# A third transfer buffer for the weights' conversion, an earlier and thinner interleaving of the first mixture, and phi(q) on ScalarE

## The chip, the cores and the metric

The kernel runs on one core of one Trainium2 chip. A core has TensorE (PE: matrix products; PEld is its weight load), VectorE (DVE), ScalarE (ACT), GpSimd (POOL) and SyncE (SP), which here issues nearly all transfers. They run in parallel, each through its own list of instructions in a fixed order, and wait for one another on semaphores. The metric is the time of one execution on the device, in microseconds (us), lower is better; the times before are three runs, of which the median counts.

## The reference

Three layers follow each other. Attention over 2 batches of 8 heads, 576 tokens and 64 columns per head joins causal softmax attention with a lookup in a memory through phi(q). Then comes a dense mixture layer with a piecewise quadratic activation, then a top-1 mixture of 8 experts with a capacity:

```
scores = where(causal, -1e9, (q @ k.T) / 8)          # per batch and head
local  = softmax(scores) @ v
phi(x) = where(x > 0, x, exp(x) - 1) + 1
mem    = (phi(q) @ M_prev) / (phi(q) @ z_prev + 1e-6)
x      = g * mem + (1 - g) * local                    # g = sigmoid(beta), x: [1152, 512]
h      = x @ w_in                                     # [1152, 2048]
x      = where(h >= 1, h, where(h <= -1, 0, (h + 1)**2 / 4)) @ w_out
e      = argmax(x @ w_gate)                           # 8 experts, capacity 288
out    = gate * (relu(x @ w1[e]) @ w2[e])
```

`w_in` and `w_out` arrive as 64-bit numbers, and the kernel converts them itself.

## The kernel before

**Attention** (`attn`) goes through 40 chunks of up to 128 queries for two heads at once. The first 20 are of batch 0 (first two chunks for each of four head pairs, then three for each), the last 20 of batch 1. A step of the generator is one third of an iteration: `softmax(i)` (scores on PE, maximum on DVE at L306 or L320, exponential on ACT at L308 or L324, reciprocal on DVE at L331, scaling on POOL at L336 and ACT at L334), then `turn(i - 1)` (transposes on PE at L355, copies on ACT at L356), then `values(i - 3)` (products with v on PE at L381; the finished block goes to `XT` on ACT at L385 and DVE at L386). `prep_a` loads a head pair, and splits keys and queries into two planes on POOL (L245) and DVE (L250). `prep_b` computes phi(q) in the tile `pf` (ACT at L262, DVE at L263 and L264) and its products with the memory on PE (L268), which need a bank of the pool `ps_m`. The tokens of the first block (`XT[0]`, 256 tokens) are ready after step 33, those of the second (`XT[1]`, 320 tokens) after step 69, and there are 129 steps.

**The weights' conversion** (`load_half`) has 8 pieces for each of four halves. A piece is a transfer of 512 KB into a buffer of the pool `st` (SP, L164), three instructions on DVE (L170 to L172, into a tile `ws`, which has two buffers), and a high and a low plane on ACT (L173) and POOL (L174). The last reader of an `st` buffer is L172; after it SP may issue the next transfer into that buffer.

**The first mixture**: `moe0(bi)` takes a block through the first half of the layer: eight steps of `layer1` (12 products at L429 into a bank of `ps_m`; ACT at L436 and L439, DVE at L437, L438 and L440), then four steps of 24 products with `w_out` (L446) and a store. Blocks 0 and 1 are interleaved with attention. Blocks 2 and 3 (`moe0s`) follow it, beside the conversion of the second halves, whose space is free only when attention's tiles are.

The order in which an engine gets its instructions is set before the run: `mix(a, b, ra, rb)` takes ra steps of a and rb steps of b in turn, and a scheduler then places each instruction by its own estimate of when its inputs are there. On the chip nothing changes place any more, so an instruction that waits holds everything behind it on its engine. `m` and `hp` are banks of `ps_m`, of which there are two.

Of the kernel before, what the change touches and what calls it, by code (L numbers as in the profile page):

```python
# [13 lines left out]
AF = mybir.ActivationFunctionType  # L14
ALU = mybir.AluOpType
# [37 lines left out]
def f(ap):  # L53
    return ap.bitcast(F32)
# [3 lines left out]
def kernel(ctx: ExitStack, tc: tile.TileContext, kd, kq_d, qx_d, v_d, mz_d,  # L58
                              betap, betab, w_in, w_out, w_gate, w1, w2, cap, out):
    nc = tc.nc  # L60
    ACT, DVE, POOL, PE, SP = nc.scalar, nc.vector, nc.gpsimd, nc.tensor, nc.sync
# [15 lines left out]
    def bank(p, tag):  # L77
        return p.tile([128, 512], F32, tag=tag, name=tag)
# [45 lines left out]
    def setup_late():  # L124
        POOL.memset(wg, 0.0)
        SP.dma_start(out=wg[:, :, :NE], in_=w_gate.rearrange("(k p) e -> p k e", p=128))

        for e in range(2):
            o = 2 * e * FEW
            DVE.tensor_tensor(out=summing[:, e * FEW:(e + 1) * FEW], in0=ident[:, o:o + FEW],  # L130
                              in1=ident[:, o + FEW:o + 2 * FEW], op=ALU.add)
        POOL.memset(onesb, 1.0)
        POOL.memset(upper, 1.0)
        POOL.affine_select(out=upper, in_=upper, pattern=[[1, 128]], compare_op=ALU.is_gt,
                           fill=0.0, base=0, channel_multiplier=-1)
        for e in range(NE):
            POOL.memset(rev[:, e:e + 1], float(NE - e))
# [7 lines left out]
    def wtile(slot, j, planes=True):  # L145

        shape, dt = ([128, 2, 4, 512], F32R) if planes else ([128, 4096], F32)
        return pools[slot].tile(shape, dt, tag=f"w{slot}{j}", name=f"w{slot}{j}")

    def load_half(half, key):  # L150

        if key == "in":
            src = w_in.bitcast(I32)[:, half * 2048:(half + 1) * 2048].rearrange("(k p) f -> p k f", p=128)
        else:
            src = w_out.bitcast(I32)[half * 1024:(half + 1) * 1024, :].rearrange("(k p) d -> p k d", p=128)
        ts = [wtile(slot_of[key, half], j) for j in range(2)]
        wt[key, half] = ts
        for i in range(8):  # L160
            j, k = divmod(i, 4)
            t = ts[j]
            r = st.tile([128, 512, 2], I32, tag="st", name="st")
            d = SP.dma_start(out=r.rearrange("p a b -> p (a b)"),  # L164
                             in_=src[:, k, j * 1024:(j + 1) * 1024] if key == "in" else src[:, i, :])
            if (key, half) == ("in", 0) and i < NPIN:
                tc.keep_in_program_order(d)
            lo, hi = r[:, :, 0], r[:, :, 1]
            s = tp.tile([128, 512], I32, tag="ws", name="ws")
            DVE.tensor_scalar(s, hi, 3, 0x3FFFFFFF, op0=ALU.logical_shift_left, op1=ALU.bitwise_and)  # L170
            DVE.scalar_tensor_tensor(out=s, in0=hi, scalar=-0x40000000, in1=s, op0=ALU.bitwise_and, op1=ALU.bitwise_or)  # L171
            DVE.scalar_tensor_tensor(out=s, in0=lo, scalar=29, in1=s, op0=ALU.logical_shift_right, op1=ALU.bitwise_or)  # L172
            ACT.activation(out=t[:, 0, k, :], in_=f(s), func=AF.Copy)  # L173
            POOL.tensor_tensor(out=t[:, 1, k, :], in0=f(s), in1=f(t[:, 0, k, :]), op=ALU.subtract)  # L174
            yield

    def rows_of(n):

        return [(r, c0, c1) for r, c0, c1 in ((128, 0, 2), (64, 2, n)) if c0 < c1]
# [18 lines left out]
    def qcols(a, b):  # L198
        return slice(a, b) if b <= CUT else slice(S + a, S + b)

    def attn(P):
# [51 lines left out]
        def prep_b(vi, si):  # L253

            b, pr, subs = visits[vi]
            t = T[vi]
            mz = t["mz"]
            sub = SUBS[si]
            q0, q1 = CH[sub[0]][0], sum(CH[sub[-1]])
            qr = t["kq"][:, qcols(q0, q1)]  # L260
            pf = qp.tile([128, 320], F32, tag="pf", name="pf", bufs=1)[:, :q1 - q0]
            ACT.activation(out=pf, in_=qr, func=AF.Exp)  # L262
            DVE.tensor_scalar(pf, pf, 1.0, None, op0=ALU.min)  # L263
            DVE.scalar_tensor_tensor(out=pf, in0=qr, scalar=0.0, in1=pf, op0=ALU.max, op1=ALU.add)  # L264
            nps = bank(ps_m, "m")
            for i, ci in enumerate(sub):
                o, m = CH[ci]
                PE.matmul(nps[:m, i * 130:i * 130 + 130], pf[:, o - q0:o - q0 + m], mz, start=True, stop=True)  # L268
            nv = nps[:, :390].rearrange("p (c x) -> p c x", c=3)
            rn = mp.tile([128, 3, 2], F32, tag="rn", name="rn")  # L270
            xm = mp.tile([128, 3, 128], F32, tag="xm", name="xm")
            for r, c0, c1 in rows_of(len(sub)):
                gb = gall[:r, 2 * pr:2 * pr + 2].unsqueeze(1).to_broadcast([r, c1 - c0, 2])
                DVE.scalar_tensor_tensor(out=rn[:r, c0:c1], in0=nv[:r, c0:c1, 128:130], scalar=1.0e-6, in1=gb, op0=ALU.add, op1=ALU.mult)
                DVE.reciprocal(rn[:r, c0:c1], rn[:r, c0:c1])
                DVE.tensor_tensor(out=xm[:r, c0:c1].rearrange("p c (h d) -> p c h d", h=2),  # L276
                                  in0=nv[:r, c0:c1, :128].rearrange("p c (h d) -> p c h d", h=2),
                                  in1=rn[:r, c0:c1].unsqueeze(3).to_broadcast([r, c1 - c0, 2, 64]), op=ALU.mult)
            t["xm", si] = xm
# [339 lines left out]
    def head(g, n):  # L619
        for _ in range(n):  # L620
            if next(g, 0) == 0:
                return
            yield

    def mix(a, b, ra, rb):

        a, b = iter(a), iter(b)
        la = lb = True
        while la or lb:
            for _ in range(ra):  # L630
                la = la and next(a, 0) != 0
            for _ in range(rb):
                lb = lb and next(b, 0) != 0
# [302 lines left out]
    side = ExitStack()  # L936
# [1 line left out]
    def spool(name, bufs):  # L938
        return side.enter_context(tc.tile_pool(name=name, bufs=bufs, side="right"))

    st = ctx.enter_context(tc.tile_pool(name="st", bufs=2, side="right"))
    g1 = ExitStack()
    ga = pool("ga", GA)
    gb = g1.enter_context(tc.tile_pool(name="gb", bufs=5))
# [2 lines left out]
    cmask2 = P[2].tile([128, 64], BF16, name="cmask2", bufs=1)  # L947
    setup(cmask, cmask2)
    at = attn(P)
    mix(head(at, 39), chain(load_half(0, "in"), load_half(0, "out")), 5, 2)  # L950
    setup_late()
    route_init()
    m0 = moe0(0)
    mix(head(at, 24), head(m0, 8), 3, 1)
    mix(head(at, 12), m0, 4, 1)
    m1 = moe0(1)
    mix(at, head(m1, 9), 9, 1)
    m0 = chain(moe0s(2, ga), moe0s(3, ga))
    next(m0)
    run(m1)  # L960
# [101 lines left out]
```

## Time and profile before

| what | value |
|---|---|
| median of 3 runs (lowest, highest) | 452.03 us (449.75, 453.09) |
| the profiled execution's own time | 446.63 us |
| its span | 444.9 us |
| PE busy | 410.1 us, 92% of the span |
| DVE, ACT, POOL busy | 289.6, 208.2, 140.2 us |
| mean granted clock of TensorE | 0.969 of full speed |

The trace comes from one execution. The slices of the page show PE at nine tenths or more after some 245 us, and below that in the first half, where attention, the first mixture and the conversion run side by side; the clock that was granted falls to a half for some microseconds in a few places there. Busy time of PE includes the modelled ends of its products, so a busy PE isn't yet a PE at its peak.

### The profile page before, as it was taken

The numbers are of one execution on the slowest core, as the hardware profiler recorded it, in microseconds if no ns is written. First come the engines' busy times: TensorE is split into PE (matmuls) and PEld (weight loads), VectorE is DVE, ScalarE is ACT, GpSimd is POOL, SyncE is SP. The second block draws the span as 40 slices with busy tenths as digits, with TensorE's granted clock in tenths as the row PEclk, the third lists the DMA queues.
The fourth block names the chain that finished last, engine by engine and source line by source line (L and its number), as shares of the span: only waits on it lengthen the run. The fifth ranks groups of instructions, "written<-read, shape, count | busy, mean of one in ns | idle before, by whom it ended". The sixth has DMA issues, their size and how long they took to land. (4 is left out here: it accounts for less than half of the span.)

```text
span 444.9 us, 8598 instructions
## 1 busy us (share of the span) xinstructions
PE 410.1 (92%) x3023; PEld 343.8 (77%) x3024; DVE 289.6 (65%) x921; ACT 208.2 (47%) x587; POOL 140.2 (32%) x161
## 2 busy tenths in 40 slices
PE   8997878979699999999888999999989999999993
PEld 4553565857488787888887999998987989989951
DVE  5459979898957877588789444445554756557230
ACT  3667664868543877674334323223444323132121
POOL 4127748665633252144425000000276200200002
PEclk9899968999899999999969999999999999999998
DMA  4176772846576540006542300300544303993001
GB/s 124 50 230 219 245 245 87 325 138 226 165 249 250 159 133 7 2 18 194 172 151 96 96 1 1 118 1 25 166 147 163 96 1 133 334 315 134 14 1 56
DMA packets 30414, 58.79 MB, mean 132 GB/s; under 512 B 3549, under 2 KB 15197, under 8 KB 30370
## 3 DMA queue, kind: packets, MB, share of 16 engines
q1 hardware_dynamic: 27986, 49.44, 34.2%
q0 software_dynamic: 2384, 8.80, 6.1%
q8 instruction: 24, 0.39, 0.3%
q14 instruction: 20, 0.16, 0.1%
HBM read 50.53 MB, written 7.80 MB: 131 GB/s over the span
## 5 line engine op out<-in xcount | busy, mean ns | idle before, releaser
L429 PE MATMUL hp<-xt,win 128*128 128x256 f32 (+1 forms) x768 | 118.2, 302 | 2.2 <-DVE xm L276 1.3
L429 PEld LDWEIGHTS hp<-xt,win 128*128 128x128 f32 x768 | 108.1, 193 | 3.4 <-DVE xm L276 1.6
L437 DVE SCALAR_TENSOR_TENSOR hp<-hp,w 128x256 f32<-128x256 f32 (+1 forms) x64 | 29.5, 461 | 47.1 <-ACT w L436 46.9
L336 POOL TENSOR_SCALAR a<-a,rs 128x128 f32<-128x128 f32 (+4 forms) x40 | 29.0, 726 | 88.0 <-DVE rs L331 65.3
L446 PE MATMUL s<-g,wx 128*128 128x256 f32 (+1 forms) x288 | 49.8, 301 | 1.6 <-ACT g L439 1.6
L436 ACT ACTIVATE w<-hp 128x256 f32<-128x256 f32 (+1 forms) x64 | 26.3, 412 | 52.3 <-PE hp L429 50.9
L439 ACT ACTIVATE g<-hp 128x256 fp32r<-128x256 f32 (+1 forms) x64 | 26.2, 410 | 41.5 <-DVE hp L438 41.5
L446 PEld LDWEIGHTS s<-g,wx 128*128 128x128 f32 x288 | 41.7, 189 | 4.5 <-ACT g L439 2.1
L440 DVE TENSOR_TENSOR g<-hp,g 128x256 fp32r<-128x256 f32 (+1 forms) x64 | 29.0, 453 | 22.2 <-ACT g L439 22.0
L381 PE MATMUL x<-at,v 128*64 128x128 f32 (+2 forms) x480 | 42.9, 275 | 0.4 <-ACT at L356 0.3
L356 ACT ACTIVATE at<-t 128x512 f32<-128x512 f32 (+3 forms) x80 | 33.7, 435 | 18.8 <-PE t L355 18.7
L306 DVE TENSOR_SCALAR_CACHE_REDUCE skip<-s 128x128 bf16<-128x128 f32 (+3 forms) x64 | 30.8, 481 | 14.9 <-PE s L303 14.3
L355 PE MATMUL t<-ident,a 128*128 128x128 f32 (+1 forms) x200 | 35.5, 290 | 4.3 <-ACT at L356 2.7
L308 ACT ACTIVATE a<-s,nm 128x128 f32<-128x128 f32 (+3 forms) x64 | 33.7, 527 | 11.7 <-DVE skip L306 10.2
L381 PEld LDWEIGHTS x<-at,v 128*64 128x64 f32 (+1 forms) x480 | 28.5, 142 | 13.3 <-issue 3.7
L726 POOL TENSOR_TENSOR win<-ew,win 128x512 fp32r<-128x512 f32 x8 | 10.1, 1292 | 77.3 <-ACT win L725 77.3
L446 PE MATMUL s<-g,wout 128*128 128x256 f32 (+1 forms) x144 | 26.3, 312 | 4.8 <-ACT g L439 3.9
L355 PEld LDWEIGHTS t<-ident,a 128*128 128x128 f32 (+1 forms) x200 | 22.2, 144 | 10.4 <-issue 7.1
L438 DVE SCALAR_TENSOR_TENSOR hp<-w,hp 128x256 f32<-128x256 f32 (+1 forms) x64 | 29.3, 458 | 1.3
L446 PE MATMUL op<-g,wout 128*128 128x256 f32 (+1 forms) x192 | 29.4, 301 | 0.0
L172 DVE SCALAR_TENSOR_TENSOR ws<-st,ws 128x512 int32<-128x512 int32 x32 | 28.3, 886 | 0.2
L171 DVE SCALAR_TENSOR_TENSOR ws<-st,ws 128x512 int32<-128x512 int32 x32 | 27.8, 868 | 0.3
(212 smaller groups left out, 769.3 us busy)
## 6 DMA issues: line engine op xcount, KB each, us to landing
st<-in_w_in_dram SPq DMA_DIRECT2D x16, 512.0 KB, 4.6
st<-in_w_out_dram SPq DMA_DIRECT2D x16, 512.0 KB, 3.5
hi<-in_kd_dram POOLq DMA_DIRECT2D x4, 1152.0 KB, 6.1
ew<-in_w_dram SPq DMA_DIRECT2D x8, 512.0 KB, 3.3
win<-in_w_dram SPq DMA_DIRECT2D x8, 512.0 KB, 4.7
wx<-in_w_dram SPq DMA_DIRECT2D x8, 512.0 KB, 6.2
hi<-in_kd_dram POOLq DMA_DIRECT2D x3, 896.0 KB, 8.1
kq<-in_kq_dram SPq DMA_DIRECT2D x4, 576.0 KB, 4.5
```

Source lines behind the costliest of these rows:

```text
L172: DVE.scalar_tensor_tensor(out=s, in0=lo, scalar=29, in1=s, op0=ALU.logical_shift_right, op1=ALU.bitwise_or)
L306: DVE.tensor_scalar(skip[:, :K], sps[hh][:, :K], -0.125, None, op0=ALU.mult, op1=ALU.min, accum_out=nm[:, hh:hh + 1])
L308: ACT.activation(out=x[:, :K], in_=sps[hh][:, :K], func=AF.Exp, scale=0.125, bias=nm[:, hh:hh + 1], accum_out=rs[:, hh:hh + 1])
L336: POOL.tensor_scalar(x[:, :K], x[:, :K], rs[:, j:j + 1], 1.0, op0=ALU.mult, op1=ALU.mult)
L355: PE.transpose(tp_[:r, (c - c0) * 128:(c - c0) * 128 + 128], x[:, c * 128:c * 128 + r], ident)
L356: ACT.activation(out=(at2 if c0 else at[:, :c1]).rearrange("p a b -> p (a b)"), in_=tp_[:r, :(c1 - c0) * 128], func=AF.Copy)
L381: PE.matmul(xps[hh * 64:hh * 64 + 64, o - q0:o - q0 + m], t["v"][:r, c, hh * 64:hh * 64 + 64], src, start=False, stop=(last and c == ci))
L429: PE.matmul(hp[:, :n], wi[:, a, k, cs], xt[:, x, k, :], start=(k == 0 and i == 0), stop=(k == KD - 1 and i == 2))
L437: DVE.scalar_tensor_tensor(out=u, in0=u, scalar=2.0, in1=w[:, :n], op0=ALU.mult, op1=ALU.max)
L438: DVE.scalar_tensor_tensor(out=u, in0=w[:, :n], scalar=2.0, in1=u, op0=ALU.min, op1=ALU.mult)
L440: DVE.tensor_tensor(out=g[:, 1, :n], in0=u, in1=f(g[:, 0, :n]), op=ALU.subtract)
L446: PE.matmul(op, wo[:, a, c % 4, d * 128:(d + 1) * 128], g[:, x, :n], start=(c == 0 and i == 0), stop=(c == 7 and i == 2))
```

## The change

```
-            ACT.activation(out=pf, in_=qr, func=AF.Exp)
-            DVE.tensor_scalar(pf, pf, 1.0, None, op0=ALU.min)
+            ACT.activation(out=pf, in_=qr, func=AF.Relu, scale=-1.0)
+            ACT.activation(out=pf, in_=pf, func=AF.Exp, scale=-1.0)
             DVE.scalar_tensor_tensor(out=pf, in0=qr, scalar=0.0, in1=pf, op0=ALU.max, op1=ALU.add)
...
-    st = ctx.enter_context(tc.tile_pool(name="st", bufs=2, side="right"))
+    st = ctx.enter_context(tc.tile_pool(name="st", bufs=3, side="right"))
...
-    mix(head(at, 39), chain(load_half(0, "in"), load_half(0, "out")), 5, 2)
+    mix(head(at, 33), chain(load_half(0, "in"), load_half(0, "out")), 2, 1)
     setup_late()
     route_init()
     m0 = moe0(0)
     mix(head(at, 24), head(m0, 8), 3, 1)
-    mix(head(at, 12), m0, 4, 1)
+    mix(head(at, 12), m0, 3, 1)
     m1 = moe0(1)
-    mix(at, head(m1, 9), 9, 1)
+    mix(at, head(m1, 9), 6, 1)
```

phi(q) keeps its value: exp(min(q, 0)) was min(exp(q), 1), and is now exp(-relu(-q)). A minimum on DVE goes, 16 times, and ACT gets one more instruction each time. The 16 pieces of the conversion now go beside 32 steps of attention, one after each two, where it was two after each five. Block 0 of the first mixture starts at step 33 in place of 39, and block 1 at step 69 in place of 75; block 1 gets a step for six of attention's in place of nine.

What this does to the order shows in three places. The first is SP's queue while attention is in batch 1: the last transfers into `st` of the first halves (`w_in` and `w_out` by name), the loads of attention (`v`, `mz`, `qw`, `kq`), and the writes of zeros to the output. Before:

```order
L222 DMA kq<-in_kq_dram 128x1152
L164 DMA st<-in_w_out_dram 128x1024 x4
L228 DMA v<-in_v_dram 128x4x128
L230 DMA v<-in_v_dram 64x128
L224 DMA mz<-in_mz_dram 128x130
L164 DMA st<-in_w_in_dram 128x1024
L240 DMA qw<-in_qx_dram 128x576
L222 DMA kq<-in_kq_dram 128x1152
L525 DMA x2d<-zr 1x512
L527 DMA out_dram<-zr 128x512 x9
L164 DMA st<-in_w_in_dram 128x1024 x2
```

And in the change:

```order
L164 DMA st<-in_w_out_dram 128x1024 x2
L164 DMA st<-in_w_in_dram 128x1024
L228 DMA v<-in_v_dram 128x4x128
L230 DMA v<-in_v_dram 64x128
L164 DMA st<-in_w_in_dram 128x1024
L222 DMA kq<-in_kq_dram 128x1152
L240 DMA qw<-in_qx_dram 128x576
L164 DMA st<-in_w_in_dram 128x1024
L525 DMA x2d<-zr 1x512
L527 DMA out_dram<-zr 128x512 x9
L164 DMA st<-in_w_in_dram 128x1024
```

Three transfers of the second half's `w_in` stand ahead of the zeros, where there was one, and each stands ahead of loads of attention that it followed.

The second place is PE around the last products with v (L381), where `op` (L446) are block 1's output products and `s` and `x` block 2's. Before:

```order
L446 MATMUL op<-g,wout_633 128x320 x3
L429 MATMUL hp<-xt_1731,win_269 128x256 x12
L381 MATMUL x<-at,v 64x64 x8
L381 MATMUL x<-at_2647,v 64x64 x2
L446 MATMUL op<-g,wout_632 128x320 x12
L446 MATMUL op<-g,wout_633 128x320 x12
L446 MATMUL s<-g,wout_632 128x256 x3
L446 MATMUL x<-g,wout_632 128x256
```

And in the change:

```order
L381 MATMUL x<-at,v 64x128 x7
L355 MATMUL t<-ident,a 64x128
L446 MATMUL op<-g,wout_516 128x320 x9
L446 MATMUL s<-g,wout_515 128x256 x3
L446 MATMUL op<-g,wout_515 128x320 x5
L381 MATMUL x<-at,v 64x64 x8
L381 MATMUL x<-at_2707,v 64x64 x2
L446 MATMUL op<-g,wout_515 128x320 x7
L446 MATMUL op<-g,wout_516 128x320 x12
```

Up to the last product with v the kernel before has issued 204 products of L429 and 120 of L446, the change 204 and 152; behind it stand 76 of L446 before, and 43 now, ahead of the next `layer1`. At the scores of chunk 28 the counts of L429 are 96 before and 108 now, at equal counts of L446.

The third place is DVE at the same time: the last residue of attention (L386, `xt3`) among the conversion's instructions, of which each piece has its own `ws`. Before:

```order
L437 SCALAR_TENSOR_TENSOR hp_2779<-hp_2779,w_2792 128x256
L172 SCALAR_TENSOR_TENSOR ws_3273<-st_3271,ws_3273 128x512
L438 SCALAR_TENSOR_TENSOR hp_2779<-w_2792,hp_2779 128x256
L386 SCALAR_TENSOR_TENSOR xt3_1896<-x_2657,cpair_89,xt3_1896 128x320
L170 TENSOR_SCALAR ws_3345<-st_3343 128x512
L440 TENSOR_TENSOR g_2793<-hp_2779,g_2793 128x256
L171 SCALAR_TENSOR_TENSOR ws_3345<-st_3343,ws_3345 128x512
L172 SCALAR_TENSOR_TENSOR ws_3345<-st_3343,ws_3345 128x512
```

And in the change:

```order
L170 TENSOR_SCALAR ws_3201<-st_3199 128x512
L440 TENSOR_TENSOR g_2793<-hp_2779,g_2793 128x256
L171 SCALAR_TENSOR_TENSOR ws_3201<-st_3199,ws_3201 128x512
L170 TENSOR_SCALAR ws_3273<-st_3271 128x512
L172 SCALAR_TENSOR_TENSOR ws_3201<-st_3199,ws_3201 128x512
L171 SCALAR_TENSOR_TENSOR ws_3273<-st_3271,ws_3273 128x512
L172 SCALAR_TENSOR_TENSOR ws_3273<-st_3271,ws_3273 128x512
L170 TENSOR_SCALAR ws_3345<-st_3343 128x512
L171 SCALAR_TENSOR_TENSOR ws_3345<-st_3343,ws_3345 128x512
L386 SCALAR_TENSOR_TENSOR xt3_1916<-x_2717,cpair_89,xt3_1916 128x320
L172 SCALAR_TENSOR_TENSOR ws_3345<-st_3343,ws_3345 128x512
```

The residue now comes behind an L440, an L170 and an L171 that it preceded. From there to the conversion's last L172 both lists hold the same five `layer1` and the same nine pieces that follow.

## Rows read from the trace of the kernel before

**Rows 1.** Busy us by stage: stretch, length, engines, granted clock, DMA share, GB/s.

```profile
35.00:60.00 25.00, 17.38 (x121) 11.49 (x120) 24.91 (x68) 16.61 (x47) 18.92 (x20) 0.98 0.68 210
60.00:125.00 65.00, 55.67 (x441) 42.86 (x441) 57.60 (x153) 42.90 (x128) 38.58 (x40) 0.90 0.60 198
125.00:205.00 80.00, 79.17 (x659) 64.68 (x657) 55.81 (x177) 53.65 (x166) 27.47 (x31) 1.00 0.38 122
205.00:245.00 40.00, 35.16 (x240) 33.36 (x237) 35.52 (x57) 13.52 (x31) 17.01 (x12) 0.91 0.45 144
```

**Rows 2.** Waits of DVE, 35 to 125 us: total us, times, longest.

```profile
DVE ws L170 <- DMA st<-in_w_in_dram: 2.7, 1, 2.7
DVE ws L170 <- DMA st<-in_w_out_dram: 2.6, 1, 2.6
```

**Rows 3.** Timeline, 104 to 116 us: start, us, engine, line, tile [idle before <-releaser].

```profile
105.72 2.95 SPq L164 DMA_DIRECT2D st<-in_w_out_dram  x2
...
107.30 1.01 DVE L172 SCALAR_TENSOR_TENSOR ws<-st,ws 128x512 int32<-128x512 int32 x1
...
111.75 0.43 DVE L170 TENSOR_SCALAR ws<-st 128x512 int32<-128x512 int32 x1 [2.61 <-DMA st<-in_w_out_dram]
...
113.70 1.86 PE L268 MATMUL m<-mz,pf 128*128 128x130 f32 x6 [2.55 <-DVE g L440]
```

**Rows 4.** Busy time of short stretches, columns as in the stages.

```profile
60.00:65.00 5.00, 5.00 (x35) 3.79 (x35) 2.26 (x5) 4.10 (x15) 0.93 (x1) 0.50 1.00 356
...
150.00:155.00 5.00, 5.00 (x44) 4.34 (x43) 4.42 (x19) 5.00 (x16) 1.62 (x4) 1.00 0.32 94
220.00:225.00 5.00, 2.08 (x11) 1.74 (x11) 3.65 (x8) 1.56 (x4) 1.26 (x1) 0.79 0.56 181
225.00:230.00 5.00, 5.00 (x26) 5.00 (x26) 4.12 (x8) 1.79 (x4) 1.33 (x1) 0.53 0.42 124
```

**Rows 5.** Groups by form, 35 to 125 us: busy us, mean ns, idle before.

```profile
L263 DVE TENSOR_SCALAR pf<-pf 128x256 f32<-128x256 f32 x2 | 1.6, 822 | 0.5 <-ACT pf L262 0.5
L263 DVE TENSOR_SCALAR pf<-pf 128x320 f32<-128x320 f32 x4 | 1.6, 392 | 0.0
```

**Rows 6.** Lines L263 and L262: count, ns min/median/max, first and last start.

```profile
L263 DVE TENSOR_SCALAR pf<-pf x16: 260/314/1350, 4.0 to 168.8; 128x256 f32<-128x256 f32 x8, 128x320 f32<-128x320 f32 x8
...
L262 ACT ACTIVATE pf<-kq x16: 402/436/499, 3.6 to 166.9; 128x256 f32<-128x256 f32 x8, 128x320 f32<-128x320 f32 x8
```

**Rows 7.** Timeline, 116 to 121 us.

```profile
118.54 1.43 POOL L174 TENSOR_TENSOR wout<-ws,wout 128x512 fp32r<-128x512 f32 x1
118.76 1.35 DVE L263 TENSOR_SCALAR pf<-pf 128x256 f32<-128x256 f32 x1
```

**Rows 8.** Timeline of PE, 192 to 209 us.

```profile
192.79 2.00 PE L429 MATMUL hp<-xt,win 128*128 128x320 f32 x12
...
205.00 3.79 PE L446 MATMUL op<-g,wout 128*128 128x320 f32 x24
```

**Rows 9.** Timeline of DVE, 208 to 244 us.

```profile
208.20 0.54 DVE L386 SCALAR_TENSOR_TENSOR xt<-x,cpair,xt 128x320 fp32r<-128x320 f32 x1
208.66 0.41 DVE L170 TENSOR_SCALAR ws<-st 128x512 int32<-128x512 int32 x1
209.00 0.41 DVE L440 TENSOR_TENSOR g<-hp,g 128x256 fp32r<-128x256 f32 x1
209.33 1.44 DVE L171 SCALAR_TENSOR_TENSOR ws<-st,ws 128x512 int32<-128x512 int32 x1
...
241.51 1.45 DVE L172 SCALAR_TENSOR_TENSOR ws<-st,ws 128x512 int32<-128x512 int32 x1
```

**Rows 10.** Waits of DVE, 208 to 244 us, and of PE, 40 to 60 us.

```profile
DVE ws L170 <- DMA st<-in_w_out_dram: 1.0, 3, 0.6
...
DVE ws L170 <- DMA st<-in_w_in_dram: 0.5, 1, 0.5
...
PE m L268 <- DVE pf L264: 1.2, 1, 1.2
```

## The prediction, made before the result was known

> **What bounds the kernel now.** Read the stages first: for each stretch, how much of it PE and DVE are busy, and at what granted clock [rows 1]. Each of the two engines is full in another place. From 35 to 60 us DVE works 24.91 of 25 us and PE only 17.38; from 60 to 125 us DVE 57.60 of 65 and PE 55.67. Here DVE's list sets the pace. From 125 to 205 us PE is busy for 79.17 of 80 us at the full clock and DVE for 55.81: PE sets the pace. From 205 to 245 us neither is full, with 35.16 and 35.52 of 40, because DVE converts the second halves and PE waits for it. What comes later is PE's alone and holds nothing that the change touches except the buffers of the experts' weights, which the change gives one more; I put that at nothing, between a gain and a loss of 0.5 us, since PE's own work covers those loads.
>
> Then ask what DVE waits for where it is the bound. In the first two stages it is one thing above all: twice, for 2.7 and 2.6 us, a piece's first instruction (L170) waits for its transfer [rows 2]. The timeline shows why. The transfer is issued at the end of SP's entry at 105.72 us, that is at 108.3, when L172 of the piece two before has ended, and DVE needs it at once: L170 starts at 111.75 after 2.61 us. DVE takes nothing past it, so L440 behind it is late, a bank of `ps_m` stays taken, and PE's L268 starts at 113.70 after 2.55 us of idleness [rows 3]. One late transfer thus stops both engines.
>
> **The change, part by part.**
>
> *The third buffer.* A transfer may now start when the piece three before is done, one piece (L170 to L172 and what stands between) earlier. From the issue at 108.3 us to L170 at 111.75 are 3.5 us, and the two waits are shorter than that, so the earlier start covers them: 2.7 + 2.6 = 5.3 us in the stretch that DVE bounds [rows 2], and 1.0 + 0.5 = 1.5 us in the last [rows 10]. The ends: nothing, and all of it. On SP more of these transfers now stand ahead of attention's loads and of the zeros, and each waits for DVE. Attention's loads are issued six chunks before use; that hides it. Without this cover the next head pair would start late by such a wait, up to 2.7 us [rows 2].
>
> *The minimum goes.* From 35 to 125 us DVE does six of them for 1.6 + 1.6 = 3.2 us [rows 5]. The five before 35 us and the five after 125 us lie where DVE isn't the bound and count nothing. One of the six took 1.35 us and ended with an instruction of POOL that had started just before it [rows 7]. The Trainium skill's page "SBUF — State Buffer", section "Who interferes with whom", says that a DVE instruction in a two-port mode or with two SBUF inputs and a GpSimd instruction exclude each other for a whole instruction. By that rule the next one, L264 with two SBUF inputs, would take over the wait, and the six would be worth their median of 0.31 us each, 1.9 in place of 3.2 us. I keep the 3.2.
>
> *The new instruction on ACT.* 16 more of L262's kind, median 0.44 us [rows 6], 7.0 us in all, of which six, or 2.6 us, in the DVE-bound stages. ACT has room there (42.90 busy of 65) but works in order, and its exponentials feed DVE. The ends are nothing and 2.6 us; I take 2.6, since phi(q) must now pass ACT twice before PE's L268.
>
> First stages together: 5.3 + 3.2 - 2.6 = **5.9 us** less, out of PE's idle time there, 7.6 + 9.3 = 16.9 us [rows 1], so PE can follow. The ends are 0 and 8.5.
>
> *The first mixture earlier and thinner.* The number of products stays; their place changes. At the scores of chunk 28, where PE becomes the bound, 12 products of L429 more are done (in gaps that PE had). From there to the last product with v, PE has 12 of L429 less and 32 of L446 more, by the counts in the order. Twelve of L429 took 2.00 us and 24 of L446 3.79 [rows 8]: 32 x 0.158 - 2.0 = 5.05 - 2.0 = **3.0 us** more in the PE-bound stage. The `layer1` work on ACT and DVE that comes along is covered there (DVE 55.81 of 80).
>
> *What comes back after attention.* From L386 at 208.20 us to the end of the last L172 at 242.96 DVE sets the pace. The change has L170, L440 and L171 of this stretch ahead of L386: 0.41 + 0.41 + 1.44 = 2.3 us less [rows 9]. With the landings' 1.5 us that is 3.8 us, and PE's 33 output products fewer behind attention leave it with just enough to do until the next `layer1` is through DVE. The ends are 0 and 3.8; I take **3.0**, as some of DVE's time there is waiting for ACT and PE.
>
> The sum: - 5.9 + 3.0 - 3.0 = -5.9 us. The profiled execution took 446.63 us, so it would take 440.7; it is 5.4 us quicker than the median of the runs, 452.03, from which I forecast **446.1 us**. The ends: -8.5 + 3.0 - 3.8 = -9.3 and +3.0 with a loss of 0.5 later.
>
> **The rivals.**
>
> *The clock comes along* (chance 0.20). After an idle stretch TensorE is granted the lower of its two levels (1.2 in place of 2.4 GHz) for some us: from 60 to 65 us the clock is at 0.50, at 220 to 230 us at 0.79 and 0.53 [rows 4], which is 2.5 + 1.05 + 2.35 = 5.9 us of lost PE time. If the gaps go, so does this: 446.1 - 5.9 = 440 us. For it: each stretch follows a gap that hangs on DVE. Against it: from 60 to 65 us PE wasn't the engine that decided, and 33 fewer products behind attention make a gap there likelier.
>
> *The transfers are late anyway* (0.22). At the first of the two waits the DMA engines were busy for the whole of 60 to 65 us, at 356 GB/s [rows 4]. An earlier issue then only lengthens the queue, and the 5.3 and 1.5 us stay: -3.2 + 2.6 + 3.0 - 2.3 = 0.1, or 452 us. The Trainium skill's "DMA: Bandwidth & Descriptors", section "Issuing engines are not separate DMA queues", says that all transfers run interleaved on the same 16 engines, whoever starts them; by that rule the row at 60 us decides. Against it speaks the second wait: its transfer took 3.5 us from a free buffer, and the mean share in the stage is 0.60 [rows 1].
>
> *ACT becomes the engine that is waited for: slower* (0.18). The place is L268 on PE, which stands in order between the scores and the products with v. Before, it waited once for `pf`, 1.2 us [rows 10]. In the change `pf` passes ACT's queue twice, and that queue is full in stretches such as 150 to 155 us, 5.00 of 5 [rows 4]. Eleven of the 16 are later than 35 us. If each of them waits 1.2 us, that is 13.2 us: with -8.5 + 3.0 - 3.0 of the rest (its 2.6 us for ACT being in the 13.2) 452.03 + 4.7 = 456.7 us. It turns slower from the eighth such wait on (8.5 / 1.2 = 7.1).
>
> **How the numbers follow.** The forecast has 0.40. The range must leave out no more than 2 in 10: it reaches from 438, below the rival with the clock and the better ends, to 456, almost to the slower one. Of this kernel a measurement tells about 1% from no change, that is 4.5 us, with the border at 447.5. The forecast lies close to it, so its chance splits 0.28 faster, 0.12 within; the clock's rival is 0.20 faster; the late transfers are 0.20 within, 0.02 slower; ACT is 0.18 slower. That makes 0.48, 0.32 and 0.20.
>
> **What would show it.** In the profile after: DVE's waits for `st` gone in the first mixture (or still there: the second rival); PE's idle time from 35 to 125 us down by some 6 us from 16.9; the last product with v no more than 3 us late against chunk 28; L386 to the last L172 near 31 us in place of 34.8; no gap of PE over 2.9 us behind attention. Waits of PE's L268 for `pf` above 1 us, several times, would show the slower rival. The prediction would be wrong if DVE's list from 35 to 125 us took as long as before with the waits gone, since then something else in it, such as POOL's planes of attention, had set the pace.

## The result, and the profile after

The changed kernel takes 444.54 us (median of 20 runs, 440.94 to 451.28), the kernel before 448.98 (20 runs, 445.23 to 457.98). The ratio is **0.9903 [0.9879, 0.9927]**: 4.4 us faster. The forecast was 446.1 us and a gain of 5.9 us, made against the three runs that were shown then, whose median was 452.03. The ratio and all ratios below leave disturbed executions out, the medians count every run; three runs of the last experiment and four to six of some others remain in the ratio, which is why their intervals are wide and a median and its ratio can differ.

The profiled execution after has a span of 442.4 us (own time 444.1), 2.5 us less than before. The stages, which answer to [rows 1] (columns: stretch, length, busy us of PE, PEld, DVE, ACT, POOL with counts, granted clock, DMA share, GB/s):

```profile
35.00:60.00 25.00, 17.80 (x135) 13.09 (x134) 23.68 (x52) 14.92 (x44) 19.44 (x16) 0.93 0.61 196
60.00:125.00 65.00, 56.76 (x441) 44.18 (x441) 59.98 (x155) 45.10 (x133) 41.20 (x43) 0.92 0.67 215
125.00:205.00 80.00, 79.12 (x634) 64.61 (x632) 54.57 (x176) 54.45 (x169) 24.04 (x30) 1.00 0.33 107
205.00:245.00 40.00, 34.20 (x252) 32.37 (x252) 36.59 (x58) 14.08 (x32) 18.59 (x13) 0.91 0.44 143
```

In the first two stages DVE should have become emptier. It did not: 24.91 + 57.60 = 82.5 us before, 23.68 + 59.98 = 83.7 us now, with 14 instructions fewer (207 in place of 221). PE's idle time there fell from 16.9 to 7.20 + 8.24 = 15.4 us, by 1.5 and not by 6. Yet the waits that the change aimed at are gone. DVE's waits after, 35 to 125 us (total, times, longest), against [rows 2]:

```profile
DVE skip L306 <- PE s L303: 1.6, 2, 1.4
DVE rn L274 <- PE m L268: 1.4, 1, 1.4
DVE ws L170 <- POOL win L174: 1.2, 1, 1.2
DVE ws L170 <- POOL wout L174: 1.1, 1, 1.1
```

No landing of `st` is left in the list. L170 now waits for its other tile instead: `ws` has two buffers, and the older one is free only when POOL's L174 has read it. The timeline shows what fills the rest (start, length, engine, line; in brackets the idle time before and its releaser):

```profile
54.18 3.01 POOL L245 TENSOR_TENSOR kl<-kq,hi 64x576 fp32r<-64x576 f32 x2
...
54.33 1.60 DVE L250 TENSOR_TENSOR hi<-qw,hi 64x320 fp32r<-64x320 f32 x1
...
55.96 1.77 DVE L171 SCALAR_TENSOR_TENSOR ws<-st,ws 128x512 int32<-128x512 int32 x1
57.27 1.59 POOL L174 TENSOR_TENSOR win<-ws,win 128x512 fp32r<-128x512 f32 x1
57.66 1.54 DVE L250 TENSOR_TENSOR hi<-qw,hi 64x320 fp32r<-64x320 f32 x1
59.12 0.15 DVE L331 RECIPROCAL rs<-rs 128x2 f32<-128x2 f32 x1
...
59.31 0.61 ACT L334 ACTIVATE a<-a,rs 128x384 f32<-128x384 f32 x1 [4.76 <-DVE rs L331]
...
60.13 0.33 PE L381 MATMUL x<-at,v 64*64 64x64 f32 x4 [4.10 <-ACT at L356]
```

Three DVE instructions take 4.9 us; their least times are 0.42, 0.66 and 0.42 us, 1.5 together. Each ends 0.2 to 0.5 us behind the POOL instruction that was running when it started (the two L245 take half of 3.01 us each). A DVE instruction drawn out like this is called held below. The time counts as busy, not as a wait, so no view of waits names it. The tiny reciprocal L331 behind them keeps ACT idle for 4.76 us and PE for 4.10. The sum over 35 to 125 us shows in DVE's groups there (count, busy us, mean ns, idle us before them and its releasers). Before:

```profile
L250 DVE TENSOR_TENSOR hi<-qw,hi 64x320 fp32r<-64x320 f32 (+1 forms) x14 | 13.9, 1013 | 0.2
L172 DVE SCALAR_TENSOR_TENSOR ws<-st,ws 128x512 int32<-128x512 int32 x15 | 13.3, 884 | 0.0
L171 DVE SCALAR_TENSOR_TENSOR ws<-st,ws 128x512 int32<-128x512 int32 x15 | 11.2, 745 | 0.0
L170 DVE TENSOR_SCALAR ws<-st 128x512 int32<-128x512 int32 x14 | 7.1, 506 | 5.3 <-DMA st<-in_w_in_dram 2.7 <-DMA st<-in_w_out_dram 2.6
```

After:

```profile
L250 DVE TENSOR_TENSOR hi<-qw,hi 64x320 fp32r<-64x320 f32 (+1 forms) x14 | 15.8, 1150 | 0.2
L171 DVE SCALAR_TENSOR_TENSOR ws<-st,ws 128x512 int32<-128x512 int32 x15 | 14.9, 992 | 0.1
L172 DVE SCALAR_TENSOR_TENSOR ws<-st,ws 128x512 int32<-128x512 int32 x14 | 11.1, 790 | 0.0
L170 DVE TENSOR_SCALAR ws<-st 128x512 int32<-128x512 int32 x15 | 9.7, 645 | 2.3 <-POOL win L174 1.2 <-POOL wout L174 1.1
```

The lines of these instructions over the whole kernel after, and L263, which answers to [rows 5, 6] (count, ns min/median/max, first and last start):

```profile
L171 DVE SCALAR_TENSOR_TENSOR ws<-st,ws x32: 660/693/2008, 30.1 to 239.2; 128x512 int32<-128x512 int32 x32
...
L250 DVE TENSOR_TENSOR hi<-qw,hi x22: 418/1298/1696, 37.8 to 166.2; 64x320 fp32r<-64x320 f32 x14, 64x256 fp32r<-64x256 f32 x8
...
L245 POOL TENSOR_TENSOR kl<-kq,hi x14: 1395/1506/1739, 38.9 to 164.1; 64x576 fp32r<-64x576 f32 x14
...
L263 ACT ACTIVATE pf<-pf x16: 406/444/475, 4.0 to 175.4; 128x256 f32<-128x256 f32 x8, 128x320 f32<-128x320 f32 x8
```

Where the 2.5 us of the profiled pair come from is read from three marks on DVE: the start of the last L306 of chunk 28 (the 28th, with 384 keys), the last L386, the last L172. Before, the first mark was this row, and the other two are [rows 9]:

```profile
145.27 0.56 DVE L306 TENSOR_SCALAR_CACHE_REDUCE skip<-s 128x384 bf16<-128x384 f32 x1
```

After:

```profile
144.93 0.55 DVE L306 TENSOR_SCALAR_CACHE_REDUCE skip<-s 128x384 bf16<-128x384 f32 x1
...
212.16 0.55 DVE L386 SCALAR_TENSOR_TENSOR xt<-x,cpair,xt 128x320 fp32r<-128x320 f32 x1
...
240.45 1.12 DVE L172 SCALAR_TENSOR_TENSOR ws<-st,ws 128x512 int32<-128x512 int32 x1
```

Up to the first mark the gain is 0.3 us. From there to L386 the changed kernel loses 4.3 (62.9 to 67.2), from L386 to the end of the last L172 it gains 5.4 (34.8 to 29.4), and behind that 1.1 more: 0.3 - 4.3 + 5.4 + 1.1 = 2.5 us. The marks do not stand for equal work on PE: at the first, the changed kernel has done 12 products of L429 more, which take some 2 us by [rows 8]. Behind attention PE's gap has grown from 2.92 to 4.13 us, and the low clock around it has stayed (0.79 and 0.53 before [rows 4]):

```profile
223.03 1.01 PE L446 MATMUL s<-g,wout 128*128 128x256 f32 x3 [4.13 <-ACT g L439]
```

```profile
220.00:225.00 5.00, 1.72 (x6) 1.42 (x7) 5.00 (x8) 1.29 (x3) 2.28 (x2) 0.64 0.66 234
225.00:230.00 5.00, 5.00 (x32) 5.00 (x32) 4.67 (x10) 1.92 (x4) 1.50 (x2) 0.68 0.39 121
```

### The profile page after: what moved, and what is told of

Read it like the earlier page. It is cut to its first block, busy times and chain, and to the rows that moved or that the text cites. A ratio compares the mean times of both kernels' runs of the same rounds, so it can differ in the third digit from the quotient of the medians.

```text
span 442.4 us, 8597 instructions
## 1 busy us (share of the span) xinstructions
PE 409.4 (93%) x3023; PEld 344.7 (78%) x3024; DVE 289.3 (65%) x905; ACT 213.1 (48%) x603; POOL 141.9 (32%) x161
## 5 line engine op out<-in xcount | busy, mean ns | idle before, releaser
L429 PE MATMUL hp<-xt,win 128*128 128x256 f32 (+1 forms) x768 | 120.1, 304 | 1.8 <-DVE g L440 1.8
L429 PEld LDWEIGHTS hp<-xt,win 128*128 128x128 f32 x768 | 108.6, 193 | 4.0 <-DVE g L440 2.1
L336 POOL TENSOR_SCALAR a<-a,rs 128x128 f32<-128x128 f32 (+4 forms) x40 | 29.4, 736 | 83.8 <-DVE rs L331 49.3
L446 PE MATMUL s<-g,wx 128*128 128x256 f32 (+1 forms) x288 | 49.5, 300 | 1.2 <-ACT g L439 1.2
L381 PE MATMUL x<-at,v 128*64 128x128 f32 (+2 forms) x480 | 42.9, 271 | 4.6 <-ACT at L356 4.5
L446 PEld LDWEIGHTS s<-g,wx 128*128 128x128 f32 x288 | 41.8, 189 | 3.5 <-ACT g L439 1.6
L440 DVE TENSOR_TENSOR g<-hp,g 128x256 fp32r<-128x256 f32 (+1 forms) x64 | 28.8, 451 | 22.9 <-ACT g L439 22.7
L356 ACT ACTIVATE at<-t 128x512 f32<-128x512 f32 (+4 forms) x80 | 34.5, 437 | 13.2 <-PE t L355 12.8
L306 DVE TENSOR_SCALAR_CACHE_REDUCE skip<-s 128x128 bf16<-128x128 f32 (+3 forms) x64 | 30.9, 483 | 13.8 <-PE s L303 12.8
L381 PEld LDWEIGHTS x<-at,v 128*64 128x64 f32 (+1 forms) x480 | 27.8, 138 | 13.9 <-ACT at L356 6.2
L446 PE MATMUL op<-g,wout 128*128 128x256 f32 (+1 forms) x192 | 30.7, 304 | 3.2 <-DVE xm L276 3.2
L446 PE MATMUL s<-g,wout 128*128 128x256 f32 (+1 forms) x144 | 25.7, 308 | 5.8 <-ACT g L439 4.7
L446 PEld LDWEIGHTS op<-g,wout 128*128 128x128 f32 x192 | 26.5, 188 | 5.5 <-DVE xm L276 3.3
L171 DVE SCALAR_TENSOR_TENSOR ws<-st,ws 128x512 int32<-128x512 int32 x32 | 30.5, 953 | 0.3
```

Source lines behind the costliest of these rows:

```text
L306: DVE.tensor_scalar(skip[:, :K], sps[hh][:, :K], -0.125, None, op0=ALU.mult, op1=ALU.min, accum_out=nm[:, hh:hh + 1])
L336: POOL.tensor_scalar(x[:, :K], x[:, :K], rs[:, j:j + 1], 1.0, op0=ALU.mult, op1=ALU.mult)
L356: ACT.activation(out=(at2 if c0 else at[:, :c1]).rearrange("p a b -> p (a b)"), in_=tp_[:r, :(c1 - c0) * 128], func=AF.Copy)
L381: PE.matmul(xps[hh * 64:hh * 64 + 64, o - q0:o - q0 + m], t["v"][:r, c, hh * 64:hh * 64 + 64], src, start=False, stop=(last and c == ci))
L429: PE.matmul(hp[:, :n], wi[:, a, k, cs], xt[:, x, k, :], start=(k == 0 and i == 0), stop=(k == KD - 1 and i == 2))
L440: DVE.tensor_tensor(out=g[:, 1, :n], in0=u, in1=f(g[:, 0, :n]), op=ALU.subtract)
```

## The experiments

**Theory A** after the first look: DVE's two-input instructions (L171, L172, L250, L264) are held by POOL's two-input ones (L245, L174), and what the change freed on DVE in stage 1 went into longer holds. **Theory B**: the order in which the scheduler puts the work, and the two buffers of `ws`, decide, and the holds cost either kernel the same.

### The three parts, alone and left out

Each part alone, put into the kernel before:

```diff
-    st = ctx.enter_context(tc.tile_pool(name="st", bufs=2, side="right"))
+    st = ctx.enter_context(tc.tile_pool(name="st", bufs=3, side="right"))
```

> The kernel before with a third transfer buffer and nothing else. Theory (held instructions): the 5.3 and 1.5 us that DVE waits for transfers go, but a part comes back as waits for a free ws tile and as DVE instructions held behind POOL, as in the changed kernel (2.3 and 2.7 us of such waits, 6 us more in the conversion and in L250): a gain of 0 to 2 us, ratio 0.996 to 1.0. Rival (the buffer is the whole of the gain): a ratio of 0.990 or below.

Measured: 446.51 us, ratio 0.9953 [0.9917, 0.9989], a little more than the theory's 0.996 to 1.0 and less than the rival's.

```diff
-            ACT.activation(out=pf, in_=qr, func=AF.Exp)
-            DVE.tensor_scalar(pf, pf, 1.0, None, op0=ALU.min)
+            ACT.activation(out=pf, in_=qr, func=AF.Relu, scale=-1.0)
+            ACT.activation(out=pf, in_=pf, func=AF.Exp, scale=-1.0)
```

> The kernel before with phi(q) by two instructions of ACT and nothing else. Theory: DVE loses 3.2 us in the stages that it bounds, ACT's longer way costs less than that: a gain of 1 to 3 us, ratio 0.993 to 0.998. Rival (ACT becomes the engine that is waited for): ratio 1.005 or above, with waits of PE's L268 for pf.

Measured: 451.61 us, ratio 1.0057 [1.0013, 1.0100], slower. Here the wait of the slower rival shows, twice between 35 and 125 us, on PE:

```profile
40.83 0.71 PE L268 MATMUL m<-mz,pf 128*128 128x130 f32 x4 [2.00 <-DVE pf L264]
...
52.19 1.08 PE L268 MATMUL m<-mz,pf 128*128 128x130 f32 x6 [1.06 <-DVE pf L264]
```

```diff
-    mix(head(at, 39), chain(load_half(0, "in"), load_half(0, "out")), 5, 2)
+    mix(head(at, 33), chain(load_half(0, "in"), load_half(0, "out")), 2, 1)
...
-    mix(head(at, 12), m0, 4, 1)
+    mix(head(at, 12), m0, 3, 1)
...
-    mix(at, head(m1, 9), 9, 1)
+    mix(at, head(m1, 9), 6, 1)
```

> The kernel before with the new interleaving and nothing else. Theory: 3.0 us more in the stage that PE bounds and some 4 us less behind it, with two buffers still and the transfers' waits still there: ratio 0.996 to 1.002. Rival (the interleaving is the whole of the gain): 0.990 or below.

Measured: 449.62 us, ratio 1.0019 [0.9985, 1.0054], as the theory has it.

The product of the three ratios is 1.003, and the three together give 0.9903: the parts do not add. So each was also left out of the changed kernel, with the same lines turned back.

> The changed kernel with the old phi(q): ACT's Exp alone and DVE's minimum (line 263) again. Alone the new phi cost 2.6 us against the kernel before. Theory A (hold: with three buffers DVE is the one that attention waits for, and the minimum is one instruction more that can be held): the time rises by 1 to 3 us over the changed kernel (445.5 to 447.5), the minimum takes over 0.8 us between 35 and 125 us. Theory B (the second activation lengthens the chain to phi more than the minimum did, as the run of this part alone suggests): the time falls by 1 to 3 us, 441.5 to 443.5, and line 263 starts sooner after ACT's line 262.

Measured: 449.59 us, ratio 1.0001 [0.9964, 1.0038]. Theory A had the sign but not the size: by the ratios 1.0001 and 0.9903 the loss against the changed kernel is 4.4 us, where it allowed 1 to 3; and the minimum, which it put above 0.8 us, has a median of 0.31 us between 35 and 125 us, with 1.53 as the longest of five.

> The changed kernel with the old mixing (5:2 from step 39, 4:1, 9:1). Alone the new mixing was worth nothing measurable (ratio 1.002). Theory A (the pace of the conversion decides which pieces meet POOL's planes of attention, and the third buffer needs the steadier mixing): the time rises by 1.5 to 3 us over the changed kernel to about 446.5, that of the buffer alone, and the last line 172 of stage 3 ends 31 us or more behind line 386. Theory B (the mixing does nothing): the time stays within 1 us of the changed kernel.

Measured: 444.94 us, ratio 0.9892 [0.9851, 0.9934]. The mixing is worth nothing in this company either. Its profile shows why. Its marks answer to the three above:

```profile
147.75 0.55 DVE L306 TENSOR_SCALAR_CACHE_REDUCE skip<-s 128x384 bf16<-128x384 f32 x1
...
208.77 0.55 DVE L386 SCALAR_TENSOR_TENSOR xt<-x,cpair,xt 128x320 fp32r<-128x320 f32 x1
...
242.35 1.11 DVE L172 SCALAR_TENSOR_TENSOR ws<-st,ws 128x512 int32<-128x512 int32 x1
```

With the old mixing chunk 28 to L386 takes 61.0 us and L386 to the last L172 34.7; with the new one 67.2 and 29.4. The mixing moves 5 to 6 us from behind attention to in front of its end, so that what it saves later is paid there. The first mark lies 2.8 us behind that of the changed kernel here, and 2.5 us behind that of the kernel before, although this kernel is as fast as the changed one: a gain up to chunk 28 depends on the order, and does not tell by itself what buffer and phi are worth.

> The changed kernel with two transfer buffers again (phi by ACT and the new mixing stay). The buffer alone gave a ratio of 0.995, the phi alone 1.006, the mixing alone 1.002. Theory A (the buffer carries the whole gain, and the rest is order): the waits of line 170 for the landing of st come back, 3 to 6 us between 35 and 125 us, and the time is that of the kernel before, 448 to 451. Theory B (the phi and the mixing carry it): the time stays below 446.

Measured: 447.24 us, ratio 0.9950 [0.9921, 0.9979], between the two expectations. The landings' waits are back, though only 1.8 + 0.9 = 2.7 us of them.

With the kernel before and the changed one these are all eight combinations. Each part then has four differences of ratios, one in each company of the other two (in per cent, negative is faster):

| part | with neither | with one of the others | with both | mean |
|---|---|---|---|---|
| buffer | -0.47 | phi -1.65, mixing -0.18 | -0.47 | -0.69 |
| phi by ACT | +0.57 | buffer -0.61, mixing -0.69 | -0.98 | -0.43 |
| mixing | +0.19 | buffer +0.48, phi -1.07 | +0.11 | -0.07 |

A mean rests on the kernel before and seven ratios whose intervals are 0.2 to 0.4% to either side; by that it is known to about 0.3%. In us: the buffer 3.1, the phi 1.9, the mixing 0.3, each give or take 1.2. The single differences reach from -1.65 to +0.57, more than their intervals allow: in another company the same part meets another order of instructions. A part tried alone says little here; the phi alone has the wrong sign.

### POOL's reading instructions

First, the weights' low plane without POOL's subtraction:

```diff
-            POOL.tensor_tensor(out=t[:, 1, k, :], in0=f(s), in1=f(t[:, 0, k, :]), op=ALU.subtract)
+            for _ in range(2):
+                POOL.memset(f(t[:, 1, k, :]), 0.0)
```

> The changed kernel, with the low planes of the first mixture's weights left out: POOL's L174 reads nothing and writes zeros twice in place of the difference, so its output is that of rounded weights. Theory (POOL's reading instructions hold DVE's): L170 to L172 return to about 0.41, 0.69 and 0.69 us each; in the changed kernel they take 35.0 us from 35 to 125 us in place of some 27, and 36.9 from 195 to 245 in place of 25: up to 19 us of DVE's time in stretches that it bounds, and a gain of 6 to 15 us against the changed kernel, ratio to the kernel before 0.957 to 0.977. Rival (the order and PE's own work set the time): 0.985 to 0.995.

Measured: 446.34 us, ratio 0.9947 [0.9913, 0.9982]. That is the rival's range, but it does not tell the theories apart. The memsets wait for nothing, so they moved to the start, among POOL's first instructions for attention: up to 35 us POOL has 22.57 us in place of 11.05, and PE, the first column of busy times, only 28.61 in place of 33.66.

```profile
0.00:35.00 35.00, 28.61 (x126) 15.18 (x127) 21.40 (x92) 17.71 (x66) 22.57 (x66) 0.90 0.29 79
```

So the edit was made again with memsets that keep the old place, because they write the tile that ACT has just read:

```diff
-            POOL.tensor_tensor(out=t[:, 1, k, :], in0=f(s), in1=f(t[:, 0, k, :]), op=ALU.subtract)
+            POOL.memset(f(s), 0.0)
+            POOL.memset(f(s), 0.0)
...
-    PASS3 = ((0, 0), (0, 1), (1, 0))
+    PASS3 = ((0, 0), (0, 1), (0, 0))
```

> The changed kernel in which POOL's subtraction of line 174 (two operands read from SBUF) is replaced by two memsets of the same ws tile, which wait for the same ACT copy and free the tile at about the same time, and the product with the weights' low plane is replaced by a second product with the high plane, so that TensorE has as many products (it leaves the low planes out). Theory A (the gain of stage 1 was given back because DVE's two-input instructions are held behind POOL's two-input ones): lines 171 and 172 fall from 14.23 and 11.05 us between 35 and 125 us to about 0.70 us each (10.5 each for 15), the waits of line 170 for ws stay near 3, DVE's list between 35 and 125 us gets some 3 to 4 us shorter, and the time falls by 1 to 4 us under the changed kernel (about 441 to 443.5). Theory B (the ws buffers and the order set the pace): lines 171 and 172 may fall, but DVE then waits in their place for ws or for PE, and the time stays within 1 us of the changed kernel, 443.5 to 445.5.

Measured: **427.97 us, ratio 0.9498 [0.9447, 0.9548]**, by the ratios some 18 us under the changed kernel, more than four times the most that theory A priced. POOL's two memsets take 0.53 us each, 1.05 together, where the subtraction takes 1.27 at least; but they read nothing. L171 with them:

```profile
L171 DVE SCALAR_TENSOR_TENSOR ws<-st,ws x32: 633/681/1277, 29.7 to 220.7; 128x512 int32<-128x512 int32 x32
```

L171's longest falls from 2.01 to 1.28 us, and the last one starts at 220.7 in place of 239.2 us. From 35 to 125 us the 16 of L171 and of L172 take 0.71 and 0.77 us on the mean, where the 15 and 14 of the changed kernel took 0.99 and 0.79. The larger part lies behind 195 us, where attention's L245 is over and L174 alone is left on POOL to hold them. There L172 in the changed kernel, and with the memsets:

```profile
L172 DVE SCALAR_TENSOR_TENSOR ws<-st,ws 128x512 int32<-128x512 int32 x14 | 15.4, 1100 | 0.2
```

```profile
L172 DVE SCALAR_TENSOR_TENSOR ws<-st,ws 128x512 int32<-128x512 int32 x12 | 8.2, 682 | 0.1
```

The kernel is a bound, not a version: the low planes are left out, PE no longer waits for them, and a `ws` tile is taken for a little less time. Which of these the 18 us belong to is not separated here.

Then versions that compute everything. The keys' low plane on DVE:

```diff
-                POOL.tensor_tensor(out=kl[r, hh, :KE], in0=kq[r, kcols(0, KE)], in1=f(hi[r, hh, kcols(0, KE)]), op=ALU.subtract)
+                DVE.tensor_tensor(out=kl[r, hh, :KE], in0=kq[r, kcols(0, KE)], in1=f(hi[r, hh, kcols(0, KE)]), op=ALU.subtract)
```

> The changed kernel with line 245 (the low plane of the keys, 64x576 with two SBUF operands, 14 of 1.5 us on POOL) written by DVE, so that POOL and DVE no longer write attention's planes side by side. Theory A (hold): line 250 falls from 1.30 us (median, 22 of them) to about 0.45, 19 us less DVE in the whole of attention, and the 14 of line 245 cost DVE about 0.7 each, 10 us more; DVE's list is some 9 us shorter up to 170 us, the gap of 4.10 us in front of PE's line 381 at 60 us shrinks to 2 or less, and the time falls by 2 to 5 us under the changed kernel (440 to 442.5). Theory B (line 250 takes its 1.3 us for another reason, such as its operands' planes): line 250 stays above 1 us, DVE has 10 us more, and the time rises by 2 to 5 us over the changed kernel (446 to 450).

Measured: 442.75 us, ratio 0.9803 [0.9748, 0.9857]. This expectation's theory B falls by these two lines (same columns as above):

```profile
L245 DVE TENSOR_TENSOR kl<-kq,hi x14: 730/752/1822, 49.3 to 175.9; 64x576 fp32r<-64x576 f32 x14
...
L250 DVE TENSOR_TENSOR hi<-qw,hi x22: 407/482/875, 50.4 to 177.0; 64x320 fp32r<-64x320 f32 x14, 64x256 fp32r<-64x256 f32 x8
```

L250 falls from 1.30 to 0.48 us (median) when L245 leaves POOL, and L245 itself takes half of what it took there. But theory A's list of DVE, 9 us shorter, does not come out of these two lines: the 14 of L245 cost DVE 12.6 us in all, and the 22 of L250 take 10.3 us in place of 22.6, 12.3 less. What did go is the gap on PE from the timeline. Its waits of L381 for ACT, from 35 to 125 us, were 4.5 us, the longest 4.1, and are now:

```profile
PE x L381 <- ACT at L356: 1.1, 2, 0.6
```

The keys' low plane, ready in half the time, and an emptier POOL may have their part in the gain; that is not separated.

Both low planes on DVE, the keys' as above and the weights':

```diff
-            POOL.tensor_tensor(out=t[:, 1, k, :], in0=f(s), in1=f(t[:, 0, k, :]), op=ALU.subtract)
+            DVE.tensor_tensor(out=t[:, 1, k, :], in0=f(s), in1=f(t[:, 0, k, :]), op=ALU.subtract)
```

> The changed kernel with line 245 and line 174 (the weights' low plane) both written by DVE, so that no POOL instruction with two SBUF operands runs while DVE converts. Theory A (hold): lines 171, 172 and 250 fall to their least times (0.68, 0.68, 0.45), 32 of line 174 at about 0.7 add 22 us to DVE, 10 in stage 1 and 10 in stage 3, the holds that go are about 5 in stage 1 and 10 in stage 3: stage 1 is then 3 to 6 us longer than with line 245 alone on DVE, stage 3 the same, and the time is 443 to 448. Theory B (what costs is POOL's 1.4 us between ACT's plane and the free ws tile, not the hold): the shorter chain to the free tile makes the time 436 to 440.

Measured: **438.61 us, ratio 0.9731 [0.9673, 0.9788]**, the fastest version that computes everything: 2.7% under the kernel before, and 0.9731 / 0.9903 = 0.983 of the changed one. The expectation from the hold was 443 to 448 and missed; the other, 436 to 440, has the time. The holds did go, as the first says:

```profile
L170 DVE TENSOR_SCALAR ws<-st x32: 389/420/504, 29.6 to 233.7; 128x512 int32<-128x512 int32 x32
...
L171 DVE SCALAR_TENSOR_TENSOR ws<-st,ws x32: 659/682/693, 30.1 to 234.7; 128x512 int32<-128x512 int32 x32
...
L172 DVE SCALAR_TENSOR_TENSOR ws<-st,ws x32: 659/681/694, 31.3 to 236.3; 128x512 int32<-128x512 int32 x32
...
L174 DVE TENSOR_TENSOR win<-ws,win x16: 676/684/765, 34.1 to 212.8; 128x512 fp32r<-128x512 f32 x16
```

The longest of 32 L171 is 0.693 us where it was 2.008. DVE took on 46 instructions (951 in place of 905), some 32 us of work by their medians, and its busy time in the whole kernel went from 289.3 to 280.3 us. How much of the gain is the holds, and how much the shorter way from L173 to a free `ws` tile, which is the other expectation's reason, no run here separates. The granted clock rose as well, to 0.96 in place of 0.92 from 35 to 125 us; its share isn't separated either.

### Did the holds swallow the change?

The kernel before, with the same edits to L245 alone and to both lines:

> The kernel before, with line 245 (the low plane of the keys) written by DVE, as in the changed kernel of the run of this name. Theory A (POOL's reading instructions swallowed what the change frees on DVE): without them the change is worth what was forecast for stage 1 as well, so this run lies 6 to 9 us over the changed kernel with line 245 on DVE (442.75 us median): 446 to 449, hardly under the kernel before, because DVE's landing waits of 5.3 us stand. Theory B (the hold was worth its 4 to 5 us to either kernel and has nothing to do with the change): this run is 4 to 5 us under the kernel before as well, 443.5 to 445.5.

Measured: 451.33 us, ratio 1.0000 [0.9950, 1.0050]. In the kernel before the edit to L245 is worth nothing, in the changed one 1.0%. DVE now waits for the keys' landing with L245 at the head of its list:

```profile
DVE kl L245 <- DMA hi<-in_kd_dram: 4.0, 2, 2.9
...
DVE ws L170 <- DMA st<-in_w_out_dram: 0.3, 1, 0.3
```

Theory A expected this run to be slow because the landing waits of 5.3 us stand; they are down to 0.3 us, with two buffers still. So the time is near theory A's, and its reason is not there.

> The kernel before with lines 245 and 174 both written by DVE, so that both kernels can be compared without POOL's reading instructions (the changed one so took 438.61 us median). Theory A (they swallowed most of what the change frees in stage 1): the difference of the change is 6 to 9 us here, as it was with line 245 alone, so this run takes 445 to 448, and DVE's waits for the landings of st stand at 4 us or more between 35 and 125 us. Theory B (the hold costs either kernel the same, and the change is worth its 4.4 us with it or without): this run takes 442 to 444.

Measured: 445.00 us, ratio 0.9797 [0.9713, 0.9881]; by the ratio, 9 us under the kernel before, it is faster than either expectation. The landings' waits stand as expected, and are larger than before:

```profile
DVE ws L170 <- DMA st<-in_w_out_dram: 7.1, 2, 4.1
```

With L245 on DVE the change is worth 0.9803 / 1.0000, 2.0%, with an interval of about 0.7% to either side; that is theory A's size. With both on DVE it is worth 0.9731 / 0.9797 = 0.993, with an interval of about 0.010 to either side: between nothing and 1.7%, which holds the 1.0% of the unedited pair too. That is 3 us, nearer to theory B's 4.4 than to theory A's 6 to 9, and so few runs exclude neither. **So it is shown that the holds are there, that they go when POOL's reading instructions go, and that moving both lines is worth about 2% to either kernel. That they ate just what the change freed is supported by the size of one pair, not by its waits and not by the other pair; it stays open.**

## Why the prediction was right, and where it was not

*The time.* A gain of 5.9 us was forecast and 4.4 were measured, of the forecast's sign and within its range. The sum came out through other terms than the prediction's, so that it came this near is in part luck.

*Stage 1, minus 5.9 us: the step that failed, in size.* Its mechanism, the landing that stops DVE and PE, was right: the two waits are gone [rows 2], and with two buffers such waits are there, 2.6 to 7.1 us in five of the six kernels with two. But 5.3 us of wait are not 5.3 us of time. The profiled pair shows 0.3 us up to chunk 28; the buffer as a whole is worth 2.1 us alone and with both other parts, 3.1 on the mean, where 5.3 + 1.5 were written down. From 35 to 125 us DVE's account, by the rows above, reads: L170 to L172 take 35.7 us for 44 instructions in place of 31.6 for 44, L250 15.8 in place of 13.9 for 14, and new waits for `ws` 2.3 and for PE 3.0. That is 4.1 + 1.9 + 2.3 + 2.0 (3.0 less the 1.0 of L274 before) = 10.3 us, against 5.3 + 3.2 = 8.5 us freed; the rest of the list is shorter by about the difference, as L264 takes 3.0 us for 5 in place of 5.0 for 6. Conversion, L250 and L306 have the same counts in that stretch before and after, so DVE's work did not get ahead in it. Only later is the conversion ahead: its 18th piece is done at 133.3 us in place of 143.9, in a stage where PE, not DVE, is full. Why more instructions were held in the changed order is not shown. The prediction named this failure beforehand in its last sentence: DVE's list as long as before with the waits gone, and POOL's planes of attention as what sets the pace.

*The rule on DVE and POOL was put in the wrong place.* The prediction used [rows 7] and the Trainium skill's page "SBUF — State Buffer", section "Who interferes with whom", for the six minima alone. The section's sentence on two SBUF inputs applies as well to L171 and L172, two instructions of every piece, and to L250, and the trace agrees: 1.30 against 0.48 us for L250. It also says, and the prediction's sentence leaves out, that such an instruction does not contend with a GpSimd instruction which only writes; the memsets of the kernel without low planes agree, with L172 at 0.68 us on the mean behind 195 us, in place of 1.10.

*The phi, 3.2 less 2.6 us.* The sum of 0.6 us stands against 1.9 (give or take 1.2), so of the 2.6 us for ACT some 3.2 - 1.9 = 1.3 would be on the path by that mean: the new instruction takes 0.444 us as forecast, and that part of it lies beside other work is inferred, not shown. In the company of the other two parts the phi is worth 4.4 us and the buffer 2.1, the reverse of their order in the sum.

*Stages 2 and 3, plus 3.0 and minus 3.0 us.* Right in kind and sign, both larger: 4.3 us more to L386, 5.4 us less behind it. That they cancel is shown by the kernel without the new mixing, with 0.9892 beside 0.9903. The gap behind attention, forecast at no more than 2.9 us, grew to 4.13.

*The rivals.* The clock did not come along: 0.92 from 60 to 125 us in place of 0.90, 0.64 and 0.68 at 220 to 230. It rose in the kernel with both planes on DVE (0.96). Late transfers: no, DVE has no landing of `st` left from 35 us on; one L170 waits 1.4 us for the writes of zeros, behind 125 us, where DVE is not the bound. ACT waited for: in the change, PE's L268 has no wait for `pf` at all. In the phi alone it has 3.1 us in stage 1 and the run is slower, but the kernel without the new mixing has 2.9 us in the whole run (2.0 of them in stage 1) and is as fast as the change, so these waits do not decide.

## What to carry to other kernels

A wait removed from the engine that bounds a stage is worth its length only if what comes next on that engine is ready and runs at its least time: before pricing it, compare the mean and the longest of the instructions behind it with their minimum (the median can hide it: L171 has 0.693 us with a longest of 2.008), and look for the other engine's instruction that ends where they end. Time lost that way stands as busy time in every table, and moving the work of the *other* engine (here 46 subtractions onto the busier one) can shorten the busy time of both. Where a scheduler orders the work, judge a part by leaving it out in several companies, not by one run of it alone.

## What the runs showed of the hardware

- A subtraction with two SBUF operands costs POOL about twice what it costs DVE: 128x512 takes 1.27 against 0.66 us, 64x576 1.40 against 0.73 (least times).
- In the changed kernel the longest L171, L172 and L250 take 2.01, 1.67 and 1.70 us; with both planes on DVE 0.69, 0.69 and 0.88. L170, with one SBUF input, is held too: its longest is 2.064 us after, and 0.504 with both planes on DVE:

```profile
L170 DVE TENSOR_SCALAR ws<-st x32: 391/414/2064, 29.7 to 238.7; 128x512 int32<-128x512 int32 x32
```

- The instructions of DVE that read PSUM were not seen held: the longest L306 is 0.692 us before, after and with both planes on DVE alike.
